# Loading q and k of the first batches by casting DMAs of GpSimd, with transposes by head and a new order up to block 2

## The chip, the core and the metric

The kernel runs on one core of a Trainium2 chip. The metric is device time in microseconds (us) of one launch. The engines are TensorE (PE in the profile; its weight loads are PEld), VectorE (DVE), ScalarE (ACT), GpSimd (POOL) and SyncE (SP, which only issues DMAs). A DMA can be issued from SP, ACT or POOL; only those issued from POOL are used here to change the type of the data on the way.

## The reference

q, k and v have the shape (8 batches, 8 heads, 576 positions, 64). Each head has two attentions, whose sum is the result; a two-layer network with an ELU follows on 4608 tokens of 512 values (512 to 2048 to 512).

```python
q_d = q.reshape(B, H, Sd, 4, D).mean(axis=3)      # k_d, v_d alike; Sd = 144
out_up = np.repeat(softmax_attention(q_d, k_d, v_d), 4, axis=2)
mask = np.abs(pos[:, None] - pos[None, :]) < 4
scores = np.where(mask, 0.125 * q @ k.T, -1e9)
out_local = softmax(scores) @ v
x = (out_up + out_local).transpose(0, 2, 1, 3).reshape(4608, 512)
h = x @ w_in
g = np.where(h > 0, h, np.exp(np.minimum(h, 0)) - 1)
out = g @ w_out
```

## The kernel before

Work on attention goes by batch b (8) and pair of heads j (4 pairs). For a pair, q and k are loaded as fp32 to 96 partitions by 2 heads by 6 runs by 64 (`load_qk`, lines 146 to 167), cast to fp16 with the two heads side by side (`cast_qk`), and transposed on PE in six chunks of 96 x 128, which puts one head on partitions 0 to 63 and the other on 64 to 127 of one PSUM tile (`transposes`, line 242). In batch 0 a further six matmuls with a constant matrix R (line 251) give the sums over four neighbours, that is the coarse q and k. PSUM goes to SBUF by `evict_q` (L264) and `evict_k` (L271) and, in batch 0, two small copies (L736, L737). From batch 3 on k is transposed by a DMA (`flip`) instead.

Then follow the scores (`masked_scores` in batch 0, which add a constant NEG on PE before ACT's exp at L338; `scores`, exp at L368 and a multiplication by MASK at L388 in later batches), the denominators (`den`, L403, L412, L444, L451), their spread over 128 partitions (`rb` in PSUM, L462 or L474, copied to `rcb`, L763 or L482), the sums of v (`vs`, L304), and the outputs (`lg`, L497 to L524), which DVE multiplies by the reciprocals (`ln`, L534 or L550). A last addition of the coarse to the fine part writes the token tile `xt` (L540 in batch 0, L570 later), on POOL or DVE by a list in the code.

The network goes over nine blocks of 512 tokens. MM1 of a block (`mm1`, L585 in block 0, L606 later) has sixteen steps: matmuls into `hp`, exp on ACT (`e`, L610), two instructions on DVE (L611, L612) that give `gt`. MM2 (`mm2`, L626) has sixteen steps too; its result leaves by ACT (L632) and SP.

The order of all of it is a list of events with due times written by hand: `at(time, fn, ...)` collects them, and a sort by time gives the program order, the same on every engine's queue. Only the order of the due times has a meaning. Batch 0 has its own table F (letters for T transposes, S and Z scores of the first and second half, D denominators, V sums of v, P spreads, O outputs, N normalising, H the part of MM1 that runs ahead, lv and lw the loads of v of batches 0 and 1, cv the casts of v, rp the loads of q and k of batch 1, wi the loads of w_in, k late constants) and FK, which counts filler matmuls on zeros (`keep`, L645, L648). Batches 1 to 3 have a table PLAN. MM1 and MM2 of blocks 0 to 3 have a start and a step each.

Events that share an engine wait for each other in that order: a DMA issue that waits for a free buffer holds up every later issue of its engine. `two` hands out PSUM slots of two banks in turn: three of them up to `close_front`, then two. In batch 0 `tq` and `tk` share the two slots of `misc`, so that the transposes of a pair wait until the pair before is evicted.

At the start (`first`, lines 650 to 664) SP issues q of pair 0 and q and k of pairs 1 and 2 of batch 0; ACT issues the identity ID, k of pair 0 and R; POOL issues NEG. q and k of pair 3 come later from SP. Pair 0 is cast in halves by ACT and DVE, and the six casts of pairs 1 to 3 are shared out by a list: q and k of pair 1 on ACT, q of 2 on POOL, k of 2 on DVE, q of 3 on POOL, k of 3 on ACT. In batch 1 all eight casts are on POOL, each with a small separating copy behind it (`apart`, L172).

Of the kernel before, what the change touches and what calls it, by code (L numbers as in the profile page):

```python
# [16 lines left out]
SD = S // 4  # L17
# [12 lines left out]
RUNS = 1  # L30
# [40 lines left out]
def kernel(  # L71
# [76 lines left out]
    def load_qk(b, j, held=False, queues=None):  # L148

        got = []  # L150
        for src, name in ((q, "q"), (k, "k")):
            a = src[b, 2 * j]
            t = sb.tile([QB, 2 * NB, D], FP32, tag=name + "32", bufs=3, name=name + "32")
            if held:
                nc.vector.memset(t[0:1, 0, 0:1], 0.0)
            runs_ = name == "q" or b < FLIP
            (nc.scalar if queues and name == "k" else nc.sync).dma_start(
                out=t[:].rearrange("p (e r) d -> p e (r d)", e=2) if runs_ else t[:],
                in_=bass.AP(
                    tensor=a.tensor, offset=a.offset,  # L160
                    ap=[[TPP * D, QB], [S * D, 2], [1, TPP * D]] if runs_
                    else [[D, QB], [QB * D, 2 * NB], [1, D]],
                ),
            )
            got.append(t)
        qk32[(b, j)] = got
# [7 lines left out]
    def cast_qk(b, j, half=False):  # L174

        got = []
        for t, name in list(zip(qk32.pop((b, j)), ("q16", "k16")))[:: 1 if b < FLIP else -1]:
            x = sb.tile([QB, NB, 2, D], FP16, tag=name, bufs=3, name=name)
# [4 lines left out]
            elif b == 0 and [2, 2, 0, 1, 0, 2][2 * j - 2 + (name == "k16")]:  # L183
                (act if [2, 2, 0, 1, 0, 2][2 * j - 2 + (name == "k16")] == 2 else dve)(out=x[:], in_=src)
            else:
                nc.gpsimd.tensor_copy(out=x[:], in_=src)  # L186
                apart(x[0:1, 0, 0, 0:1])
# [32 lines left out]
    def cast_v(b, j):  # L220
# [3 lines left out]
        if b >= RUNS:  # L224
            apart(v16[0:1, 0, 0, 0:1])
# [8 lines left out]
    def transposes(b, j, fill=(0, 0)):  # L234
# [3 lines left out]
        for x, t, name, n in zip(xs, tr_tiles(b), ("tq", "tk"), fill):  # L238
            s[name] = t
            keep(t, n)  # L240
            for c in range(NB):
                nc.tensor.transpose(  # L242
# [4 lines left out]
        if b == 0:  # L247
            for t in (s["tq"], s["tk"]):
                x = xs.pop(0)
                for c in range(TPP):  # L250
                    nc.tensor.matmul(
                        t[:, 736:1024].bitcast(FP32), x[:, c, :, :].rearrange("p e d -> p (e d)"),
                        C["R"][:, SD * (c // 2) : SD * (c // 2) + SD],
                        start=(c == 0), stop=(c == TPP - 1),
                    )
# [23 lines left out]
    def sums(b, j, x):  # L279
# [8 lines left out]
        if (b, j) == (1, 0) or (b >= RUNS and x == "k"):  # L288
# [241 lines left out]
    def normalise_half(js, g, lg):  # L530
# [7 lines left out]
        for t, a, b_, to in parts:  # L538
            eng = nc.vector if t == 0 and [0, 0, 0, 1, 0, 0, 0, 1][2 * g + js[0] // 2] else nc.gpsimd
# [6 lines left out]
    def normalise(b, j, lg):  # L546
# [14 lines left out]
        while t0 < S * (b + 1):  # L561
# [7 lines left out]
            eng = nc.vector if (b, t) == (1, 1) and [0, 0, 0, 1, 0, 0, 0, 1][4 + j] else nc.gpsimd  # L569
# [80 lines left out]
    def first():  # L650
# [116 lines left out]
    def first_v(j):  # L767
        v_first(0, j, dve if [0, 1, 0, 1][j] else act)
# [38 lines left out]
    F = dict(T=[-40.22, -40.16, -33.93, -33.13], S=[-38.63, -33.62, -33.34, -31.63], Z=[-32.71, -32.63, -32.4, -26.16], V=[-31.66, -30.84, -29.54, -26.17], P=[-29.55, -26.44, -25.1, -22.55], O=[-30.46, -25.6, -24.13, -20.55], N=[-25.77, -25.33, -22.75, -14.55], H=[-21.07, -20.28, -16.96, -14.76], lv=[-55.65, -54.27, -36.53, -31.7], cv=[-37.08, -33.24, -33.08, -27.13], lw=[-30.73, -29.44, -26.48, -13.01], rp=[-29.51, -28.21, -15.24, -13.2], D=[-32.62, -29.6, -25.74, -24.49], wi=[-33.23, -32.62, -30.61, -29.62], cf=[-27.76], k=[-54.63, -35.62, -30.55, -25.58], cq=[-54.5, -40.46, -33.4], l3=[-38.01])  # L807
    FK = dict(Tq=[1, 0, 0, 0], Tk=[0, 0, 0, 1], S=[0, 0, 3, 3], Z=[0, 0, 0, 0], P=[2, 2, 0, 3], O=[0, 0, 0, 0], D=[0, 1, 0, 0])
    for j in range(NPAIR):
# [12 lines left out]
        at(F["rp"][j], load_qk, 1, j, True)  # L822
        if j:
            at(F["cq"][j - 1], cast_qk, 0, j)
# [15 lines left out]
    MM1 = [[-14.36, 1.051, 0.555], [19.15, 0.992], [35.73, 1.022], [51.52, 1.02]]  # L840
    MM2 = [[14.98, 0.794], [34.5, 1.091], [51.68, 1.02]]
# [13 lines left out]
    def load(n):  # L855
# [14 lines left out]
    for b in range(1, B):  # L870
        p = PLAN[b]
        for j in range(NPAIR):
            n = NPAIR * (b - 2) + j
            at(p["cast"][j] - 0.1, cast_qk, b, j)
            at(p["cast"][j], cast_v, b, j)
            if b > 1:
                at(p["cast"][j] + 0.1, load, n + 3)
# [57 lines left out]
```

## Time and profile before

| | |
|---|---|
| time, median of 3 runs | 367.83 us (367.81 to 369.96) |
| profiled execution, its own time | 367.57 us |
| its span | 365.8 us |
| mean granted clock of PE | 0.967 |
| busy: PE, DVE, ACT, POOL | 343.8, 250.5, 201.2, 171.3 us |
| loads of q and k, median from issue to landing | 4.5 and 4.6 us |
| loads of w_in by GpSimd, the same | 8.2 us |

A row of the timeline or of a group names line, engine, operation and what it writes and reads (out<-in, partitions x elements). "Idle before, releaser" is the time that the engine stood still ahead of it and what ended that. The granted clock is a share of full speed. The DMA share can be over 1 for a stretch, since packets overlap.

### The profile page before, as it was taken

What the parts mean: (1) busy time and instruction counts of PE and PEld (TensorE: products, weight loads), DVE (VectorE), ACT (ScalarE), POOL (GpSimd) and SP (SyncE); (2) the same over time, 40 slices, a digit from 0 to 9 for tenths busy, and PEclk for the clock granted to TensorE, in tenths of its full rate; (3) what the DMA queues carried; (4) which work ended last, traced back from release to release, by engine and by line L of the source; (5) the groups of instructions that cost most, each with busy time, mean ns of one, the idle gap of its engine ahead of it and who ended that gap; (6) DMA issues with size and microseconds to landing.
All of it is one profiled execution on the core that took longest, in us unless ns stands there. A gap on an engine that the chain in (4) does not pass through costs nothing.

```text
span 365.8 us, 8655 instructions
## 1 busy us (share of the span) xinstructions
PE 343.8 (94%) x3394; PEld 196.0 (54%) x3394; DVE 250.5 (68%) x461; ACT 201.2 (55%) x369; POOL 171.3 (47%) x314
## 2 busy tenths in 40 slices
PE   6999788699978999999999999999999999999995
PEld 2766675465545555555555555555545544444443
DVE  1216799657787877987898789879865955555510
ACT  3474489417866576477547754764654343443421
POOL 0374788469593954792497449863410500000000
PEclk9579999969998999999999999999999999999999
DMA  8999999998798197688878797825004011001012
GB/s 205 201 173 221 221 207 219 218 197 219 164 205 183 35 239 158 146 187 187 174 165 187 162 204 164 193 68 110 30 30 116 30 46 40 30 37 49 30 59 85
DMA packets 100242, 51.17 MB, mean 140 GB/s; under 512 B 81770, under 2 KB 95178, under 8 KB 100202
## 3 DMA queue, kind: packets, MB, share of 16 engines
q1 hardware_dynamic: 97018, 45.90, 57.6%
q0 software_dynamic: 2736, 4.32, 6.8%
q8 instruction: 26, 0.43, 0.5%
q10 hardware_dynamic: 448, 0.40, 0.4%
q14 instruction: 14, 0.11, 0.1%
HBM read 42.24 MB, written 9.62 MB: 142 GB/s over the span
## 4 chain that ended last, share of the span: by engine, by line
PE 82%; DVE 9%; ACT 3%; DMA 2%; issue 2%; POOL 1%; SPq 0%; DVEq 0%; ACTq 0%
PE op L626 33%; PE hp L606 29%; PE sc L348 3%; PE hp L585 2%; PE lg L497 2%; DMA k<-in_k_dram 2%; PE tqk L242 2%; DVE gt L612 2%; DVE e L611 2%; POOL xt L570 1%; DVE pex L388 1%; ACT pex L368 1%; PE den L403 1%; DVE ln L550 1%; PE vs L304 1%
## 5 line engine op out<-in xcount | busy, mean ns | idle before, releaser
L626 PE MATMUL op<-WO,gt 128*128 128x512 f16 (+2 forms) x592 | 145.8, 375 | 0.0
L610 ACT ACTIVATE e<-hp 128x512 f16<-128x512 f32 x144 | 86.4, 602 | 101.2 <-PE hp L606 87.7
L606 PE MATMUL hp<-xt,WI 128*128 128x512 f16 x512 | 133.5, 383 | 0.6 <-POOL xt L570 0.3
L612 DVE SCALAR_TENSOR_TENSOR gt<-hp,e 128x512 f16<-128x512 f32 x144 | 99.6, 692 | 6.5
L611 DVE TENSOR_SCALAR e<-e 128x512 f16<-128x512 f16 x144 | 62.4, 433 | 44.5 <-ACT e L610 43.9
L626 PEld LDWEIGHTS <-gt 128*128 128x128 f16 x592 | 55.3, 98 | 60.9 <-issue 0.6
L606 PEld LDWEIGHTS <-WI 128*128 128x128 f16 x512 | 55.4, 115 | 49.6 <-issue 1.8
L570 POOL TENSOR_TENSOR xt<-ln 128x128 f16<-128x128 f16 (+10 forms) x62 | 37.1, 629 | 52.8 <-DVE ln L557 41.2
L368 ACT ACTIVATE pex<-sc 112x576 f16<-112x576 f32 x112 | 50.0, 530 | 13.7 <-PE sc L358 13.6
L388 DVE TENSOR_TENSOR pex<-pex,MASK 112x1152 f16<-112x1152 f16 x28 | 23.8, 849 | 15.7 <-ACT pex L368 15.7
L295 POOL TENSOR_TENSOR t<-qt 128x288 f32<-128x288 f16 x27 | 18.0, 666 | 33.7 <-ACT qt L264 33.7
L186 POOL CAST q<-q 96x768 f16<-96x768 f32 x30 | 24.7, 824 | 14.7 <-DMA q<-in_q_dram 10.5
L632 ACT COPY os<-op 128x512 f32<-128x512 f32 (+2 forms) x37 | 21.4, 579 | 18.0 <-PE op L626 17.9
L223 POOL CAST v<-v 112x768 f16<-112x768 f32 x32 | 27.1, 846 | 4.1 <-DMA v<-in_v_dram 4.1
L186 POOL CAST k<-k 96x768 f16<-96x768 f32 x28 | 23.5, 839 | 0.3
L289 DVE TENSOR_REDUCE kd<-kt 128x144 f16<-128x576 f16 x28 | 20.8, 744 | 0.7 <-ACT kt L271 0.7
L264 ACT COPY qt<-tqk 128x576 f16<-128x576 f16 x28 | 18.1, 646 | 4.5 <-PE tqk L242 4.0
L585 PE MATMUL hp<-xt,WI 128*128 128x256 f16 x128 | 15.9, 273 | 2.7 <-DVE gt L612 1.8
L348 PEld LDWEIGHTS <-kt 64*112 64x112 f16 x336 | 11.0, 128 | 12.7 <-issue 11.1
L242 PEld LDWEIGHTS <-q 96*128 96x128 f16 x192 | 12.1, 102 | 8.9 <-issue 3.9
L348 PE MATMUL sc<-qt,kt 64*112 64x96 f16 x336 | 14.8, 219 | 1.3 <-ACT kt L271 1.3
L585 PEld LDWEIGHTS <-WI 128*128 128x128 f16 x128 | 13.5, 114 | 3.3 <-issue 2.9
(104 smaller groups left out, 302.3 us busy)
## 6 DMA issues: line engine op xcount, KB each, us to landing
v<-in_v_dram SPq DMA_DIRECT2D x30, 336.0 KB, 6.3
q<-in_q_dram SPq DMA_DIRECT2D x32, 288.0 KB, 4.5
out_dram<-os SPq DMA_DIRECT2D x35, 256.0 KB, 2.1
k<-in_k_dram SPq DMA_DIRECT2D x31, 288.0 KB, 4.6
rcb<-rd SPq DMA_DIRECT2D x10, 360.0 KB, 5.4
WI<-in_moe_w_in_dram POOLq DMA_DIRECT2D x4, 512.0 KB, 8.2
WO<-in_moe_w_out_dram POOLq DMA_DIRECT2D x4, 512.0 KB, 8.1
v<-in_v_dram SPq DMA_DIRECT2D x2, 308.0 KB, 6.1
```

The lines of the kernel that those rows point to most:

```text
L186: nc.gpsimd.tensor_copy(out=x[:], in_=src)
L223: nc.gpsimd.tensor_copy(out=v16[:], in_=v32[:].rearrange("p (e c) d -> p c e d", e=2))
L348: nc.tensor.matmul(sc[e][0:KW, a : a + QB], s["kt"][r, KO - PAD + QB * c :][:, 0:KW], s["qt"][c][r], start=True, stop=True,)
L368: nc.scalar.activation(out=s["p"][0:rows, e, :, a : a + n], in_=g2(sc[0:rows], a, n), func=AF.Exp, scale=SCALE / 16 if b and a == HB else ...
L388: nc.vector.tensor_tensor(out=to, in0=to, in1=mk2, op=AB.mult)
L570: eng.tensor_tensor(out=xt(t)[:, j, t0 - TBLK * t : t1 - TBLK * t], in0=ln[:, la : la + z - a], in1=_rep4(ln[:, ga : ga + (z - a) // 4]), ...
L585: nc.tensor.matmul(FS[i][:, 256 * f : 256 * f + 256], w_in(dc, 2 * n + f), xts[0][:, dc, 256 * h : 256 * h + 256], start=(f == dc == 0), s ...
L606: nc.tensor.matmul(hp, w_in(dc, fc), xts[t][:, dc, :], start=(dc == 0), stop=(dc == DMC - 1),)
L610: nc.scalar.activation(out=e, in_=hp, func=AF.Exp)
L611: nc.vector.tensor_scalar(out=e, in0=e, scalar1=1.0, scalar2=-1.0, op0=AB.min, op1=AB.add)
L612: nc.vector.scalar_tensor_tensor(out=to, in0=hp, scalar=0.0, op0=AB.max, in1=e, op1=AB.add)
L626: nc.tensor.matmul(op_[:, a:z], gts[t][:, fc, 128 * tt : 128 * tt + 128], WO[:, fc, a:z], start=(fc == 0), stop=(fc == FCN - 1),)
```

## The change

The six tensors q and k of pairs 1 to 3 of batch 0, and all eight of batch 1, are loaded by DMAs that POOL issues and that write fp16. Such a DMA keeps the two heads one behind the other in a partition, so the pair is transposed head by head: 12 transposes of 96 x 64 into one half of the partitions each in place of 6 of 96 x 128, and in batch 0 the same for the sums by R. The casts of these tensors go. Pair 0 of batch 0 is handled as before, but k is issued from SP, and NEG is loaded by SP rather than POOL. The fp16 tiles have four buffers instead of three. Three of four xt additions of block 0's first parts are on DVE in place of one, all four copies of vd on ACT in place of two, and there are 13 fillers at the start for 12. The due times of batches 0 to 3 are new.

```diff
+    def runs_of(src, b, j):
+        a = src[b, 2 * j]
+        return bass.AP(
+            tensor=a.tensor, offset=a.offset, ap=[[TPP * D, QB], [S * D, 2], [1, TPP * D]]
+        )
+    def by_head(x):
+        return x[:].rearrange("p c e d -> p (c e d)").rearrange("p (e n) -> p e n", e=2)
+    def is_cast(b, j):
+        return b < 2 and (b, j) != (0, 0)
+    def load_cast(b, j):
+        qk16[(b, j)] = []
+        for src, name in ((q, "q16"), (k, "k16")):
+            x = sb.tile([QB, NB, 2, D], FP16, tag=name, bufs=4, name=name)
+            nc.gpsimd.dma_start(out=by_head(x), in_=runs_of(src, b, j))
+            qk16[(b, j)].append(x)
...
+                if is_cast(b, j):
+                    for e in range(2):
+                        nc.tensor.transpose(
+                            t[64 * e : 64 * e + 64, 128 * c : 128 * c + QB],
+                            by_head(x)[:, e, D * c : D * c + D], C["ID"][0:QB, 0:QB],
+                        )
+                    continue
...
+                    for e in range(2):
+                        nc.tensor.matmul(
+                            t[64 * e : 64 * e + 64, 736:1024].bitcast(FP32),
+                            by_head(x)[:, e, D * c : D * c + D], sums_of_4,
+                            start=(c == 0), stop=(c == TPP - 1),
+                        )
...
-            eng = nc.vector if t == 0 and [0, 0, 0, 1, 0, 0, 0, 1][2 * g + js[0] // 2] else nc.gpsimd
+            eng = nc.vector if t == 0 and [1, 1, 1, 0, 0, 0, 0, 1][2 * g + js[0] // 2] else nc.gpsimd
...
-        keep(t, 12)
+        keep(t, 13)
         const(id_np, "ID", nc.scalar)
-        for j in range(NPAIR - 1):
-            load_qk(0, j, queues=(j == 0))
+        load_qk(0, 0)
+        for j in range(1, NPAIR):
+            load_cast(0, j)
         const(sums_np, "R", nc.scalar)
-        const(neg_np, "NEG", nc.gpsimd)
+        const(neg_np, "NEG", nc.sync)
...
-        v_first(0, j, dve if [0, 1, 0, 1][j] else act)
+        v_first(0, j, dve if [0, 0, 0, 0][j] else act)
...
-    F = dict(T=[-40.22, -40.16, -33.93, -33.13], S=[-38.63, -33.62, -33.34, -31.63], Z=[-32.71, -32.63, -32.4, -26.16], V=[-31.66, -30.84, -29.54, -26.17], P=[-29.55, -26.44, -25.1, -22.55], O=[-30.46, -25.6, -24.13, -20.55], N=[-25.77, -25.33, -22.75, -14.55], H=[-21.07, -20.28, -16.96, -14.76], lv=[-55.65, -54.27, -36.53, -31.7], ...)
+    F = dict(T=[-41.13, -39.95, -36.66, -32.16], S=[-39.2, -35.63, -33.39, -30.84], Z=[-32.52, -32.14, -32.14, -28.4], V=[-33.32, -30.92, -30.71, -27.94], P=[-29.75, -28.02, -20.88, -18.53], O=[-30, -26.95, -20.73, -13.92], N=[-28.12, -24.72, -19.09, -13.8], H=[-24.18, -20.45, -18.09, -17.91], lv=[-52.45, -36.44, -34.49, -32.17], ...)
-    FK = dict(Tq=[1, 0, 0, 0], Tk=[0, 0, 0, 1], S=[0, 0, 3, 3], Z=[0, 0, 0, 0], P=[2, 2, 0, 3], O=[0, 0, 0, 0], D=[0, 1, 0, 0])
+    FK = dict(Tq=[1, 0, 0, 0], Tk=[0, 0, 2, 0], S=[1, 0, 2, 1], Z=[1, 0, 2, 0], P=[0, 1, 0, 0], O=[1, 4, 0, 2], D=[0, 0, 0, 0])
...
-        at(F["rp"][j], load_qk, 1, j, True)
-        if j:
-            at(F["cq"][j - 1], cast_qk, 0, j)
+        at(F["rp"][j], load_cast, 1, j)
...
-    MM1 = [[-14.36, 1.051, 0.555], [19.15, 0.992], [35.73, 1.022], [51.52, 1.02]]
+    MM1 = [[-14.19, 1.09, 0.706], [19.14, 0.992], [35.73, 1.018], [51.52, 1.02]]
...
-        1: dict(tr=[-8.501, -7.483, -3.079, -0.967], sc=[-4.069, -1.465, 0.547, 3.047], cast=[-21.27, -19.9, -10.3, -4.149], dn=[16.3], vs=[18.33], sp=[18.62, 18.82, 18.27, 18.69], out=[18.9, 18.88, 18.82, 18.95], ...),
+        1: dict(tr=[-12.21, -5.594, -1.76, -1.482], sc=[-7.07, 0.103, 0.888, 2.276], cast=[-23.96, -13.31, -12.32, 1.701], dn=[16.38], vs=[15.62], sp=[18.61, 18.14, 18.46, 18.98], out=[18.98, 18.52, 18.54, 18.99], ...),
...
-    at(F["l3"][0], load_qk, 0, 3)
-    for n, x in enumerate([-7.269, -2.453, 5.077]):
+    for n, x in enumerate([-8.454, -6.202, 3.581]):
         at(x, load, n)
```

MM2 of block 0 has the due times 14.98 + 0.794 i before and after; the due times of batches 2 and 3, of w_in and of w_out move by less.

More of the change, by code (lines that the diff above doesn't have):

```diff
@@ L29 @@
 KG, CG = 96, 24
-RUNS = 1
 KO = 16
@@ L156, in load_qk @@
             runs_ = name == "q" or b < FLIP
-            (nc.scalar if queues and name == "k" else nc.sync).dma_start(
+            nc.sync.dma_start(
                 out=t[:].rearrange("p (e r) d -> p e (r d)", e=2) if runs_ else t[:],
@@ L177, in cast_qk @@
         for t, name in list(zip(qk32.pop((b, j)), ("q16", "k16")))[:: 1 if b < FLIP else -1]:
-            x = sb.tile([QB, NB, 2, D], FP16, tag=name, bufs=3, name=name)
+            x = sb.tile([QB, NB, 2, D], FP16, tag=name, bufs=4, name=name)
             src = t[:].rearrange("p (e c) d -> p c e d", e=2)
@@ L182, in cast_qk @@
                 dve(out=x[:, :, 1, :], in_=src[:, :, 1, :])
-            elif b == 0 and [2, 2, 0, 1, 0, 2][2 * j - 2 + (name == "k16")]:
-                (act if [2, 2, 0, 1, 0, 2][2 * j - 2 + (name == "k16")] == 2 else dve)(out=x[:], in_=src)
             else:
@@ L287, in sums @@
         src = s["q"][:, 0:S] if x == "q" else s["kt"][:, KO : KO + S]
-        if (b, j) == (1, 0) or (b >= RUNS and x == "k"):
+        if (b, j) == (1, 0) or x == "k":
             nc.vector.tensor_reduce(
@@ L568, in normalise @@
             la, ga = (a + SH * h, HB + HB * h + a // 4) if by_pe(b) else (a, S + a // 4)
-            eng = nc.vector if (b, t) == (1, 1) and [0, 0, 0, 1, 0, 0, 0, 1][4 + j] else nc.gpsimd
+            eng = nc.vector if (b, t) == (1, 1) and [1, 1, 1, 0, 0, 0, 0, 1][4 + j] else nc.gpsimd
             eng.tensor_tensor(
@@ L838, in spread @@
         spread_copy(b, j, rb, copy)
-    MM1 = [[-14.36, 1.051, 0.555], [19.15, 0.992], [35.73, 1.022], [51.52, 1.02]]
-    MM2 = [[14.98, 0.794], [34.5, 1.091], [51.68, 1.02]]
+    MM1 = [[-14.19, 1.09, 0.706], [19.14, 0.992], [35.73, 1.018], [51.52, 1.02]]
+    MM2 = [[14.98, 0.794], [34.5, 1.095], [51.68, 1.02]]
     def mm1_at(t, i):
@@ L873 @@
             n = NPAIR * (b - 2) + j
-            at(p["cast"][j] - 0.1, cast_qk, b, j)
             at(p["cast"][j], cast_v, b, j)
             if b > 1:
+                at(p["cast"][j] - 0.1, cast_qk, b, j)
                 at(p["cast"][j] + 0.1, load, n + 3)
@@ L892 @@
                 at(p["out"][js[0]], pair_outputs, b, js)
-    at(F["l3"][0], load_qk, 0, 3)
-    for n, x in enumerate([-7.269, -2.453, 5.077]):
+    for n, x in enumerate([-8.454, -6.202, 3.581]):
         at(x, load, n)
-    for n, x in enumerate([-16.78, -5.044, -1.229, -0.973]):
+    for n, x in enumerate([-21.48, -3.996, 1.576, 2.844]):
         at(x, load_wo, n)
```

24 lines of the change are left out of this document (13 added, 11 removed).

## The prediction

> **What bounds the kernel now.** I read the busy times by stage first, to see where TensorE is not the limit. The columns are the stretch, its length, busy time (and instructions) of PE, PEld, DVE, ACT and POOL, the granted clock, the DMA share and GB/s.
>
> ```profile
> 50.00:60.00 10.00, 8.14 (x106) 6.79 (x103) 9.37 (x21) 9.64 (x22) 9.49 (x17) 1.00 0.98 201
> 60.00:80.00 20.00, 15.44 (x245) 9.91 (x246) 13.89 (x21) 8.49 (x16) 11.22 (x22) 0.83 1.16 218
> 80.00:100.00 20.00, 19.79 (x164) 10.53 (x164) 15.02 (x24) 14.10 (x28) 15.43 (x31) 1.00 0.85 194
> 100.00:366.00 266.00, 258.02 (x2298) 136.27 (x2296) 189.54 (x332) 142.91 (x263) 110.23 (x203) 0.99 0.50 115
> ...
> 8.00:9.00 1.00, 0.24 (x6) 0.13 (x4) 0.23 (x2) 0.49 (x1) 0.00 (x0) 0.74 1.10 270
> 22.00:23.00 1.00, 1.00 (x21) 1.00 (x20) 0.00 (x0) 0.31 (x2) 1.00 (x2) 0.94 1.26 210
> 74.00:76.00 2.00, 1.91 (x45) 1.69 (x46) 1.00 (x2) 0.76 (x1) 0.09 (x1) 0.50 1.34 190
> ```
>
> From 80 us on PE works nearly without a gap (19.79 of 20, then 258.02 of 266): what comes after 80 us is a fixed length, and the end moves only as far as its start moves. The edits lie before that. There, at 50 to 60 us, DVE (9.37), ACT (9.64) and POOL (9.49) are all full and PE is not; at 60 to 80 us PE loses 4.56 us and part of its clock. At the very start the clock falls within 8 to 9 us and is back only within 22 to 23 us.
>
> Then the chain that ended last, in order of time (start, length, what), for what sets the start:
>
> ```profile
> 1.69 7.60 DMA k<-in_k_dram
> 9.31 0.83 ACT k L184
> 10.14 0.53 ACT qt L264
> 11.56 0.64 PE tq L242 x6
> ```
>
> The load of k of pair 1 lands at 9.29. ACT casts it, and the eviction of pair 0 (L264 to L737) stands behind that cast in ACT's order and takes to 11.56, some 1.4 us. PE can start pair 1 only then, when pair 0's two PSUM tiles are free. From there PE has work without a break (1.00 of 1.00 still in the row at 22 us), so a time won at 11.56 is passed on.
>
> **The change, part by part.** *The start.* Rows of the timeline (start, length, engine, line; what ended the idle time), the bytes of 2 to 5 us, and one load on GpSimd's queue with its time to landing:
>
> ```profile
> 1.20 4.65 PE L645 MATMUL sc<-Z 128*128 128x512 f16 x12 [1.20 <-DVE v L652]
> 7.25 0.51 ACT L181 CAST k<-k 96x384 f16<-96x384 f32 x1 [1.75 <-DMA k<-in_k_dram]
> 9.06 0.88 PE L251 MATMUL tq<-R,q 96*128 96x144 f16 x6 [0.82 <-DMA R<-Rc]
> 1.23 0.70 POOL L89 DMA_DIRECT2D NEG<-NEGc  x1 [0.78 <-POOLq L919]
> ...
> DMA packets 671, 0.82 MB, mean 273 GB/s; under 512 B 158, under 2 KB 669, under 8 KB 671
> ...
> NEG<-NEGc POOLq DMA_DIRECT2D x1, 126.0 KB, 6.6
> ```
>
> Before, k of pair 0 shares the engines with q and k of pairs 1 and 2 on SP and lands at 7.2; R is queued behind it on ACT and lands at 9.06. Afterwards only q and k of pair 0 (by their shapes 288 KB each), ID (24.5) and R (81) are ahead, some 680 KB, and 820 KB had moved by 5 us here: I take k and R at about 5.3. The casting loads come later on their own: NEG, issued at 1.23, landed 6.6 us on, at 7.8. So PE ends its 12 fillers at 5.85 as before and the 13th at about 6.1, transposes q and k by 6.8 and has summed q by R at 7.4 (by the starts shown in the next fence); ACT then takes its 1.4 us with no cast ahead and frees the tiles at 8.9. q and k of pair 1 are issued at 1.2 and 1.9; with NEG's 6.6 us they land at 7.8 and 8.5, a little more with v beside them: 9.3. **PE starts pair 1 at 9.3 instead of 11.56, 2.2 us earlier.** Bounds: if R and k land as before, eviction starts at 9.8 rather than 10.05 (0.3 us); if the loads are no limit, 2.7.
>
> The casts of pairs 1 to 3 of batch 0 go (three on ACT at 0.83, one on DVE, two on POOL). SP no longer waits for a free fp32 buffer before the last q and k, so v comes earlier, and with it the loads of WI that stand behind the casts of v in POOL's order. The six issues of about 0.7 us lie on a POOL that does nothing yet (0.00 in the row at 8 us). NEG moves to SP and delays v by its 126 KB, half a microsecond at 273 GB/s, which SP's missing wait gives back.
>
> *Transposes and sums by head.* Pairs 1 to 3 of batch 0 and all of batch 1 issue twice the instructions, each for 64 output partitions. Whether two run side by side is seen in the output matmuls, which write halves too:
>
> ```profile
> 27.49 0.32 PE L517 MATMUL lg<-pex,v 112*64 112x96 f16 x6
> 27.64 0.23 PE L524 MATMUL lg<-pex,vd 96*64 96x72 f16 x4
> 44.11 0.42 PE L242 MATMUL tqk<-ID,q 96*128 96x96 f16 x6
> 44.37 0.42 PE L242 MATMUL tqk<-ID,k 96*128 96x96 f16 x6
> 12.20 0.48 PE tk L242 x6
> 12.68 0.72 PE tq L251 x6
> ...
> L517 PEld LDWEIGHTS <-v x48: 106/108/111, 27.5 to 36.2; 112*64 112x64 f16 x48
> L242 PEld LDWEIGHTS <-q 96*128 96x128 f16 x192 | 12.1, 102 | 8.9 <-issue 3.9
> ```
>
> Six halves of 96 columns take 0.15 us from start to next start (27.49 to 27.64), 25 ns each; six full ones 0.26 (44.11 to 44.37), 43 ns each. A pair of halves, 50 ns, so costs 7 more than one full: 12 halves 0.30 for 0.26. Fourteen tiles of transposes and six of sums at 0.04 are 0.8 us; batch 1's eight lie in a stretch where PE isn't the limit. I take **+0.5 us**. Low end 0. High end, one after another: at the low clock 0.48 a tile of transposes and 0.72 a tile of sums (12.20 and 12.68), 2.4 a pair, 7.2 for three pairs. [...]
>
> *DVE in the front.* Three of the four xt adds go to DVE instead of one; two copies of vd (0.42 each) go to ACT.
>
> ```profile
> L540 DVE TENSOR_TENSOR xt<-ln 128x448 f16<-128x448 f16 x1 | 1.2, 1194 | 0.0
> L570 DVE TENSOR_TENSOR xt<-ln 128x288 f16<-128x288 f16 x1 | 0.8, 755 | 0.0
> L680 DVE CAST vd<-vs 96x256 f16<-96x256 f32 x2 | 0.8, 420 | 3.4 <-PE vs L304 3.4
> L611 DVE TENSOR_SCALAR e<-e 128x512 f16<-128x512 f16 x16 | 7.4, 463 | 1.4 <-ACT e L610 1.4
> L186 POOL CAST q<-q 96x768 f16<-96x768 f32 x30 | 24.7, 824 | 14.7 <-DMA q<-in_q_dram 10.5
> ...
> 34.32 2.56 POOL L540 TENSOR_TENSOR xt<-ln 128x576 f16<-128x576 f16 x3
> 31.53 0.89 DVE L534 TENSOR_TENSOR ln<-lg,rcb 128x720 f16<-128x720 f32 x1
> 39.47 0.29 DVE L611 TENSOR_SCALAR e<-e 128x512 f16<-128x512 f16 x1 [0.74 <-ACT e L610]
> ```
>
> By the line through 288 (0.755) and 448 (1.194) elements one of 576 is 1.55: 2 x 1.55 + 1.19 - 1.19 - 0.84 = +2.3 us of DVE. Between the first ln at 31.53 and the first e at 39.47 DVE is nearly full. But the second add no longer waits for POOL (34.32, nearly 2 us after its ln), and the last ln and add now stand behind the first block of MM1 in the order, so they no longer precede e. I take **+0.7 us**, bounds -1 and +2.3.
>
> *The middle, 40 to 66 us.* POOL loses eight casts of 0.82 us (the row of L186) with their separators, over 6.6 us, and gets eight issues earlier, beside its waits for ln. The e of DVE takes 463 ns on the mean but 0.28 to 0.29 when undisturbed (39.47): 16 times the difference is 2.8 us of a full DVE, in the stretch where POOL casts nearly all the time. With two of three casts of batch 1 gone I take **-1.0 us**; bounds 0 and -2.8. What is late next there is DVE's own work, which stays.
>
> *The tail of batch 1.* These rows show the passage from MM2 of block 0 to MM1 of block 1:
>
> ```profile
> 65.58 0.66 PE L403 MATMUL den<-pex,IND 112*32 112x144 f16 x29 [1.24 <-DVE k L155]
> 68.06 1.78 ACT L368 ACTIVATE pex<-sc 112x576 f16<-112x576 f32 x4 [4.35 <-PE sc L358]
> 70.21 0.63 PE L304 MATMUL vs<-v,VR 112*32 112x128 f16 x24
> 71.81 0.62 PE L474 MATMUL rb<-rc,FOUR 16*128 16x144 f16 x12 [0.97 <-DVE rcb L482]
> 70.86 0.90 DVE L482 CAST rcb<-rb 128x720 f16<-128x720 f32 x1
> 74.93 1.89 DVE L550 TENSOR_TENSOR ln<-lg,rcb 128x720 f16<-128x720 f32 x2 [1.70 <-PE lg L505]
> 79.90 0.92 PE L606 MATMUL hp<-xt,WI 128*128 128x512 f16 x3 [0.28 <-POOL xt L570]
> ```
>
> Now all four spreads (rb) and the sums of v (vs) turn in two PSUM slots before the first outputs; the first ln is at 74.93, and the xt adds crowd behind it up to 79.90. The new due times put vs ahead of the denominators and order spread 1, 2, outputs 1, 2, spread 0, outputs 0, spread 3, outputs 3. With the first spread near 70, the copies of pairs 1 (ACT) and 2 (DVE) end by 71.8, and the first ln starts there, 3 us earlier; the other two pairs follow at a copy and an ln of 0.9 each, so the last ln ends near 77, and MM1 of block 1, at 79.90 today, can follow its xt adds some 2 us earlier. The last scores of batch 1 are also put ahead of the last MM1 block, which takes some of the 1.24 us before den. Against it: MM2 of the stretch is moved, not removed. I take **-2.2 us**; bounds -3.5 and +0.5. This holds only if ACT is free for pair 1's copy; today its exps end at 69.84 (68.06 + 1.78).
>
> Sum: -2.2 + 0.5 + 0.7 - 1.0 - 2.2 = -4.2 on the profiled execution, 367.57 us (span 365.8 and 1.77 around it): 363.4. The median of the runs shown is 367.83, 0.26 above it: **363.6**.
>
> **Rivals.** *The clock (faster).* It fell in the 8-to-9 row after PE had been idle most of 6 to 9 us, and came back at 22, although PE was full from 12 on. If PE is busy to 7.6 and again from 9.3, it may stay up or return one step sooner; the time at half clock, 8.5 to 22.1 by the shares in those two rows, is four steps of 3.4 us, if there are steps, and at half clock a step costs 1.7 us. Two steps: 363.6 - 3.4 = 360.2. One later: 365.3. [...] Against the gain: what PE does there, full for ten microseconds, did not bring the clock back. Chance 0.1.
>
> *Swallowed by DVE and ACT (no change).* If the adds cost 2.3 and DVE, full from 40 to 66 us, keeps its pace, only part of the start arrives: -2.2 + 0.5 + 2.3 - 1.0 on the front and -0.5 at the tail, 366.9. For it speaks 9.37 of 10 in 50 to 60 us. Chance 0.22.
>
> *GpSimd's queue late (no change).* If six loads on one queue queue up behind each other and v's many small packets, pair 1 starts at 12 to 13 instead of 9.3: 366.3 to 367.3. It decides when k of pair 1 lands after 11.5. Chance 0.1.
>
> *Halves one after another (slower).* 7.2 us instead of 0.5 on PE's unbroken stretch from 9.3: 370.3, and with batch 1's eight tiles at 0.26 uncovered, 372.4. It decides if a tile of 12 halves takes over 0.5 us at full clock. Against it stands 27.49 to 27.64; but that row has no transposes. Chance 0.1.
>
> **How the numbers follow.** Forecast (361.4 to 365.8) 0.48, and the rivals 0.1, 0.22, 0.1, 0.1. One per cent of 367.83 is 3.7 us, about what a measurement of this kernel can tell from no change; so faster lies below 364.15. Of the forecast 0.36 lies there, with the clock 0.46; the halves give 0.06 above 371.5 and a tail turned wrong together with late loads 0.08; the rest, 0.40, is within. The range is 360.0 to 369.0: it leaves out the serial halves and half of the clock's case.
>
> **What would show it.** The first per-head transposes near 9.3 us and no cast on ACT but pair 0's; 12 halves in 0.3 us at full clock; first e of MM1 near 37; e nearer to 0.3 us at 40 to 55; first ln of batch 1 within 7 us of its denominators and fewer half-clock slices near 75. I am wrong if pair 1 waits for a load on GpSimd's queue, if the xt adds on DVE delay e, or if the stretch from the denominators to MM1 of block 1 stays at 14 us.

## The result and the profile after

The changed kernel took 357.80 us (median of four runs, 356.68 to 358.49) against 368.89 for the kernel before beside it: ratio 0.9695, 95% interval 0.9646 to 0.9744. In three later series it gave 0.9779 (0.9740 to 0.9818), 0.9767 (0.9704 to 0.9829) and 0.9772 (0.9712 to 0.9833); that is 8.1 to 8.6 us below the kernel before by the ratio, and 8.1 to 10.3 us between the medians. All times and ratios below are of fast runs; one run of e3 (365.85 us) and one of the kernel before in the last series (572.52 us) were slow and are left out. The forecast was 363.6 with a range of 360.0 to 369.0: right in sign, with 4.2 us of gain where 8 to 11 were measured, and the range ended above the measured time.

The profiled execution took 356.68 us (span 354.8). Starts in the two profiles, in us:

| | before | after | won so far |
|---|---|---|---|
| first transposes of pair 1 | 11.56 | 9.66 | 1.9 |
| first ln of batch 0 | 31.53 | 26.56 | 5.0 |
| first e of MM1 | 38.84 | 35.75 | 3.1 |
| denominators of batch 1, first whole tile | 64.09 | 60.73 | 3.4 |
| first ln of batch 1 | 74.93 | 66.95 | 8.0 |
| MM1 of block 1 | 79.90 | 72.09 | 7.8 |
| denominators of batch 2 | 103.0 | 95.0 | 8.0 |
| end of the span | 365.8 | 354.8 | 11.0 |

Single executions differ: in three further profiles of the changed kernel (e5, e12 and e16 below) pair 1 starts at 8.8 to 9.5, the first ln comes at 24.2 to 24.8, the first e at 33.4 to 37.1, and MM1 of block 1 starts at 70.4 to 73.6.

Rows of the changed kernel's timeline for most of the right-hand starts:

```profile
8.25 0.64 ACT L298 COPY qt<-tq 128x576 f16<-128x576 f16 x1 [2.13 <-PE tq L279]
9.66 0.45 PE L263 MATMUL tq<-ID,q 96*64 96x96 f16 x12 [1.07 <-ACT qd L771]
9.91 0.45 PE L263 MATMUL tk<-ID,k 96*64 96x96 f16 x12
...
35.75 1.08 ACT L644 ACTIVATE e<-hp 128x512 f16<-128x512 f32 x2 [1.99 <-PE hp L619]
60.73 0.68 PE L437 MATMUL den<-pex,IND 112*32 112x144 f16 x32
66.95 1.72 DVE L584 TENSOR_TENSOR ln<-lg,rcb 128x720 f16<-128x720 f32 x2
72.09 0.81 PE L640 MATMUL hp<-xt,WI 128*128 128x512 f16 x3
```

The start came near its forecast (9.66 for 9.3), and twelve halves take 0.25 us (9.66 to 9.91). The place of the third gain, from 60.73 to 66.95, was forecast too. Not forecast were the front's 5 us at ln, 2 of which are gone again at the first e, and the last 3 us, which appear only after 95 us.

By stage, the kernel before first, then the changed one (columns as in the first fence of the prediction):

```profile
40.00:66.00 26.00, 21.01 (x275) 17.99 (x278) 23.75 (x50) 19.80 (x40) 20.99 (x39) 1.00 1.09 220
66.00:82.00 16.00, 13.55 (x210) 8.61 (x199) 9.18 (x11) 5.35 (x9) 9.43 (x19) 0.79 1.16 202
100.00:130.00 30.00, 26.00 (x326) 15.07 (x325) 23.43 (x36) 19.00 (x37) 22.27 (x43) 0.94 0.71 147
```

```profile
40.00:66.00 26.00, 24.07 (x360) 17.96 (x357) 21.08 (x46) 21.62 (x44) 15.83 (x29) 1.00 1.03 210
66.00:82.00 16.00, 14.07 (x176) 8.53 (x174) 12.74 (x18) 7.81 (x15) 13.19 (x26) 1.00 1.05 217
100.00:130.00 30.00, 28.42 (x345) 16.18 (x343) 24.58 (x42) 20.23 (x38) 19.45 (x37) 1.00 0.79 164
```

POOL falls from 20.99 to 15.83 us at 40 to 66, and PE rises by 3. At 100 to 130 us PE stood still for 4.0 us before and for 1.6 after: a stage that the prediction had taken for full.

The granted clock over the 40 slices of the page, before and after:

```profile
PEclk9579999969998999999999999999999999999999
```

```profile
PEclk9998999999999999999999999999999999999999
```

Counted by microsecond, the half clock took 11.94 us of TensorE's time before (8.5 to 22, 73 to 80, 110.6 to 114) and 1.71 after (31.4 to 34.6).

### The profile page after: what moved, and what is told of

It reads as the page before. It is cut to its first block, busy times and chain, and to the rows that moved or that the text cites. A ratio compares the mean times of both kernels' runs of the same rounds, so it can differ in the third digit from the quotient of the medians.

```text
span 354.8 us, 8863 instructions
## 1 busy us (share of the span) xinstructions
PE 338.6 (95%) x3520; PEld 191.6 (54%) x3520; DVE 247.1 (70%) x452; ACT 200.0 (56%) x368; POOL 167.6 (47%) x305
## 3 DMA queue, kind: packets, MB, share of 16 engines
q0 software_dynamic: 5600, 6.26, 10.6%
## 4 chain that ended last, share of the span: by engine, by line
PE 88%; DVE 5%; ACT 4%; issue 2%; DVEq 0%; ACTq 0%
PE op L660 35%; PE hp L640 31%; PE sc L382 3%; PE lg L531 2%; PE hp L619 2%; PE sc L679 2%; PE tqk L268 2%; ACT pex L402 1%; PE sc L392 1%; PE vs L338 1%; DVE ln L584 1%; DVE gt L646 1%; PE lg L539 1%; PE den L437 1%; ACT e L644 1%
## 5 line engine op out<-in xcount | busy, mean ns | idle before, releaser
L640 PE MATMUL hp<-xt,WI 128*128 128x512 f16 x512 | 132.0, 380 | 0.7 <-DVE xt L604 0.6
L645 DVE TENSOR_SCALAR e<-e 128x512 f16<-128x512 f16 x144 | 60.1, 417 | 40.2 <-ACT e L644 39.5
L640 PEld LDWEIGHTS <-WI 128*128 128x128 f16 x512 | 55.0, 114 | 48.2
L402 ACT ACTIVATE pex<-sc 112x576 f16<-112x576 f32 x112 | 50.0, 528 | 10.6 <-PE sc L392 10.5
L323 DVE TENSOR_REDUCE kd<-kt 128x144 f16<-128x576 f16 x28 | 20.8, 744 | 1.1 <-ACT kt L305 1.1
L205 POOL CAST k<-k 96x768 f16<-96x768 f32 x24 | 20.4, 848 | 0.1
L205 POOL CAST q<-q 96x768 f16<-96x768 f32 x24 | 19.7, 821 | 0.2 <-issue 0.2
L619 PE MATMUL hp<-xt,WI 128*128 128x256 f16 x128 | 17.0, 283 | 0.5 <-DVE v L217 0.4
L331 POOL TENSOR_TENSOR qd<-t 128x144 f16<-128x144 f32 x27 | 14.0, 519 | 2.1
L591 DVE TENSOR_TENSOR ln<-lg,rcb 128x576 f16<-128x576 f32 x20 | 15.0, 748 | 0.0
```

The lines of the kernel that those rows point to most:

```text
L402: nc.scalar.activation(out=s["p"][0:rows, e, :, a : a + n], in_=g2(sc[0:rows], a, n), func=AF.Exp, scale=SCALE / 16 if b and a == HB else ...
L619: nc.tensor.matmul(FS[i][:, 256 * f : 256 * f + 256], w_in(dc, 2 * n + f), xts[0][:, dc, 256 * h : 256 * h + 256], start=(f == dc == 0), s ...
L640: nc.tensor.matmul(hp, w_in(dc, fc), xts[t][:, dc, :], start=(dc == 0), stop=(dc == DMC - 1),)
L645: nc.vector.tensor_scalar(out=e, in0=e, scalar1=1.0, scalar2=-1.0, op0=AB.min, op1=AB.add)
```

## The experiments

Ratios are to the kernel before, with their 95% interval; kernels measured in one series on one chip share the runs of it (e1 to e4, e5 to e8, e9 to e12, e13 to e16, e17 and e18). "Changed" is the changed kernel; its three later ratios are those above, 0.977 on the mean. A difference to the kernel before is worked out from the ratio, one between two edited kernels from their medians. Each quoted text below is what was expected before the run.

### The loads against the order

*New loads, old order* (e3: the old F, FK, PLAN, MM1, MM2, engine lists and 12 fillers in the changed kernel) and *old loads, new order* (e4: `is_cast` False everywhere, fp32 loads and casts as before).

> Casting loads and work by head as in the changed kernel, but the due times, the fillers, and the lists of engines of the kernel before. Theory CLOCK: pair 1 starts near 9.7 us and the front gains what the clock allows, 361 to 365; a drop of the clock near 74 stays, as its order is the old one. Theory ORDER: the loads alone are worth 2 us at most, 366 to 368.

> The due times, fillers and lists of engines of the changed kernel, but all loads of q and k, their casts and the transposes of both heads at once as in the kernel before (casts of batch 1 at their old due times). Theory CLOCK: the clock falls in the front as before and stays up in the tail of batch 1; 362 to 366. Theory ORDER: the order keeps most of its gain, 358.5 to 361.5.

e3: 361.17 us (three runs, 359.35 to 362.99), 0.9870 (0.9809 to 0.9930). e4: 362.70, 0.9892 (0.9853 to 0.9930). Either alone gives about half, 4.8 and 4.0 us of 366.23; the sum, 8.8, is the whole, within the intervals. Both times lie in the range of theory CLOCK and not in that of ORDER, but the clock did not do what CLOCK says: in e4, with the old loads, it stayed up to 33 us and fell near 74. The prediction had 2.7 for the loads (-2.2 + 0.5 - 1.0) and 1.5 for the order (+0.7 - 2.2): both came out smaller than these; for the loads the interval (2.6 to 7.0) just reaches 2.7. In e4 TensorE also waited, in the middle of the front:

```profile
28.27 0.63 PE L621 MATMUL hp<-xt,WI 128*128 128x256 f16 x4
33.64 1.02 PE L621 MATMUL hp<-xt,WI 128*128 128x256 f16 x4 [3.90 <-DMA WI<-in_moe_w_in_dram]
```

### Which loads

*Batch 1's loads old* (e9) and *batch 0's loads old* (e10) in the changed kernel, and *batch 1's loads new in the kernel before* (e17). The core of the edits:

```diff
-        return b < 2 and (b, j) != (0, 0)
+        return b == 0 and j > 0          # e9: batch 1 by load_qk and cast_qk
+        return b == 1                    # e10 and e17: batch 0 as before
```

> The changed kernel with q and k of batch 1 loaded in fp32 by SP and cast by GpSimd (its transposes one whole matrix each again); batch 0 and the order stay changed. The loads alone had brought some 4.8 us. Theory A (GpSimd's eight casts in the middle are what the loads save: they stand ahead of its xt adds and of the transposes of batch 1): 2 to 3 us above the changed kernel of the same call, the middle from the first e to the denominators of batch 1 at 26 to 28 us instead of 25. Theory B (all the gain of the loads is in the start of batch 0): within 1 us of the changed kernel.

> The changed kernel with q and k of pairs 1 to 3 of batch 0 loaded in fp32 by SP and the ACT queue, cast by ACT, DVE and GpSimd as before; batch 1 and the order stay changed. Theory A (the start is worth what the prediction said, 2.2 us, and it is passed on): pair 1's transposes at 11 to 12 us and 2 to 3 us above the changed kernel of the same call. Theory B (a start that comes sooner is met by the loads of w_in or by another wait before the first block): pair 1 at 11 to 12 us, but the first e not more than 1 us later and the time within 1 us.

> The kernel before with q and k of batch 1 alone by casting DMAs of GpSimd (issued where their loads were issued, halves transposed by themselves); batch 0 and the whole order stay as before. Both new loads in the old order had given 4.1 us, and in the new order leaving out batch 1's cost 3.8 and batch 0's 2.6. Theory A (batch 1's casts on GpSimd are the larger part in any order): 2 to 4 us less than before. Theory B (in the old order those casts lie in cover, and the loads gain by batch 0 alone): within 1 us of before.

e9: 360.93, 0.9859 (0.9804 to 0.9914), 3.8 us above the changed kernel of its series (e12: 357.09, 0.9704 to 0.9829); by the ratios it is 3.4, some 3 either way. e10: 359.71, 0.9809 (0.9758 to 0.9861), 2.6 above, or 1.5 by the ratios, which is not told apart from zero. e17: 364.41, 0.9941 (0.9898 to 0.9985), 2.2 us (0.6 to 3.7) below the kernel before. So the estimates for batch 1's casts are 2 to 4 us in either order, where the prediction took 1.0; neither interval by itself leaves 1.0 out. The waits of TensorE between 36 and 67 us (engine and line; releaser: us, times, longest), first in e9, then in the kernel before:

```profile
PE sc L382 <- ACT pex L402: 1.3, 2, 0.6
PE tqk L268 <- POOL q L205: 1.1, 1, 1.1
PE tqk L268 <- POOL k L205: 0.9, 2, 0.6
```

```profile
PE hp L585 <- DVE gt L612: 1.8, 2, 1.6
PE tqk L242 <- ACT pex L368: 1.6, 2, 1.1
PE sc L348 <- ACT kt L271: 1.3, 2, 0.7
PE den L403 <- DVE k L155: 1.2, 1, 1.2
PE hp L585 <- issue: 1.0, 1, 1.0
```

In e9 the transposes of batch 1 wait 2.0 us for POOL's casts, and the stretch from the first e to the denominators of batch 1 takes 28.8 us, in which one piece of half clock (40 to 44 us, 1.7 us of loss) falls as well; in the four profiles of the changed kernel it takes 25.0 to 25.6 and has no such wait. That is how the casts cost time in the new order. In the kernel before no wait for POOL stands among these rows, and the stretch takes 25.3 us (38.84 to 64.09), in e17 26.5. How the casts cost time in the old order is open. In e10 pair 1 begins at 10.58 instead of 8.8 to 9.7, and TensorE then waits 2.3 us for w_in.

### The order, piece by piece

The *changed kernel again* (e5), with the *old order of batch 1's tail* (e6), with the *old PLAN of batches 2 and 3* (e7), and with the *old order, fillers and engine lists of batch 0* (e8).

```diff
-        1: dict(... dn=[16.38], vs=[15.62], sp=[18.61, 18.14, 18.46, 18.98], out=[18.98, 18.52, 18.54, 18.99], ...)
+        1: dict(... dn=[16.3], vs=[18.33], sp=[18.62, 18.82, 18.27, 18.69], out=[18.9, 18.88, 18.82, 18.95], ...)   # e6
```

> The changed kernel again, on the same chip as the three that follow, so that they have their comparison. Both theories: 0.9695 of before as measured, 355 to 358.5.

> The changed kernel with the old due times of denominators, sums of v, spreads and outputs of batch 1 alone. Theory TAIL (the new order of this tail keeps PE busy enough that the clock does not fall near 74, and is worth over 3 us with the clock): from den to the first MM1 of block 1 it takes 13 to 15 us instead of 11.4, the clock falls there, time 3 to 4 us above the changed kernel. Theory FRONT (the tail was slow because what came before it was late; the order by itself is worth what the prediction gave it): 1 to 2.2 us above.

> The changed kernel with the old due times of batches 2 and 3 alone. From the first MM1 of block 1 to the end the time was 285.9 us before and 282.7 after. If the new order of batch 2's spreads and outputs is the cause: 2 to 3 us above the changed kernel, with a fall of the clock near 104. If the cause is the clock's windows or loads: within 1 us of it.

> Casting loads and the new due times from batch 1 on, but the old due times and fillers of batch 0 and the old lists of engines (xt adds, vd copies). With all due times old the first e of MM1 came at 33.6 us in one execution, against 35.8 in the changed kernel. Theory FRONT: the new order of batch 0 is part of the gain, 2 us or more above the changed kernel. Rival: the front's gain is the loads' alone, 1 us below to 1 us above it.

e5: 358.83, 0.9779, less of a gain than the 0.9695 expected. e6: 360.62, 0.9819 (0.9781 to 0.9858). e7: 360.60, 0.9825 (0.9771 to 0.9880). e8: 357.96, 0.9755 (0.9705 to 0.9804). The old tail costs 1.8 us, the old plan of batches 2 and 3 costs 1.8 too, and the old order of batch 0 nothing. Each difference is known to some 2 us only, so neither 1.8 is clear of zero by its time; the profiles support the first two. From the denominators of batch 1 to MM1 of block 1, e6 takes 15.4 us and e5 11.4 (before 15.8, after 11.4). Over all twenty profiles this stretch takes 11.4 to 12.8 us in the thirteen with the new order of the tail and 13.3 to 15.8 in the seven with the old one. From there to the end of the span it takes 282.7 to 284.9 us in the thirteen with the new plan of batches 2 and 3 and 285.5 to 287.3 in the seven with the old one. At 100 to 130 us, e7 and then e5:

```profile
100.00:130.00 30.00, 27.37 (x319) 15.39 (x318) 23.44 (x38) 18.48 (x35) 20.24 (x39) 0.89 0.75 163
```

```profile
100.00:130.00 30.00, 29.07 (x336) 16.37 (x336) 23.34 (x38) 18.43 (x35) 18.95 (x37) 0.89 0.82 163
```

At the same clock, the old plan leaves TensorE idle for 2.6 us there and the new one for 0.9. The fall of the clock near 104 that was expected of e7 came in e5 too (102 to 110 us), so it does not tell the two apart.

### The clock in the front

*Three fillers for 13* in the changed kernel (e1) and *24 for 12* in the kernel before (e2): `keep(t, 3)` and `keep(t, 24)`.

> The changed kernel with 3 fillers at the start instead of 13, nothing else. Theory CLOCK (most of the gain is TensorE's granted clock: 24 us at half clock before, 3 us after): PE is cold at 8 us, the front runs at half clock to about 20 us, first e of MM1 3 us or more after 35.75, time 360 to 364. Theory ORDER (the gain comes from the order, the loads and the freed engines, and the clock costs little because PE waits for others there anyway): within 1 us of 357.8.

> The kernel before with 24 fillers at the start instead of 12, so that PE is busy to about 8.4 us while q, k and R are still on their way. Theory CLOCK: the clock does not fall at 8.5 us or falls for a shorter time, the front is 2 to 4 us shorter, time 364 to 366.5. Theory ORDER: 367.5 to 369.5, since fillers change no order and no load.

e2: 365.65, 0.9997 (0.9968 to 1.0025). The page of e2:

```profile
PEclk9999699989998999999999999999999999999999
```

The clock stays up to 36 us, the first ln of batch 0 comes at 26.85 instead of 31.53, and nothing is won: TensorE then stands still for 3.06 us at 31.8 with no releaser shown, and the half clock comes at 36 to 43 instead. The time lies in the range of theory CLOCK only because the kernel before beside it took 366.23; the ratio is what ORDER says. One profile proves little here: e14 below, which has 12 fillers, kept the clock up to 28 us as well. But the ten runs of e2 have a mean granted clock of 0.980 against 0.968 in the fifteen of the kernel before beside them, at the same time.

e1: 359.96, 0.9838 (0.9803 to 0.9873), some 2.4 us worse than the changed kernel's 0.977, which lies outside this interval (the intervals of that kernel's later series reach into it). The time is at the lower end of theory CLOCK, but the first e came at 36.02, not 3 us late. Two windows of PE alone (the granted clock stands behind PE's busy time) and four rows of the timeline of e1 hold a surprise:

```profile
8.00:12.00 4.00, 3.00 (x49) 1.00 1.30 197
12.00:16.00 4.00, 4.00 (x55) 1.00 1.08 178
```

```profile
10.18 0.92 PE L285 MATMUL tq<-R,q 96*64 96x144 f16 x12
10.89 0.93 PE L285 MATMUL tk<-R,k 96*64 96x144 f16 x12
...
22.38 0.54 PE L285 MATMUL tq<-R,q 96*64 96x144 f16 x12
22.75 0.54 PE L285 MATMUL tk<-R,k 96*64 96x144 f16 x12
```

The granted clock is 1.00. Yet twelve sums take 0.71 us (10.18 to 10.89) where they take 0.37 twelve microseconds later. TensorE runs at about half speed until 20.8 us and no column of the clock tells it; only the distance of equal groups does. The first ln is 5.2 us later than in a control (29.36 against 24.18 in e12), and about half of that reaches the end.

### Where the sooner front goes: the last quarter of w_in

In ten profiles with the new order of the front or the new loads, the second group of MM1's first block waited, for 0.4 to 5.8 us. In e4 and e10 the profile names w_in, in the others nothing. The rows of e16, a third control: the last quarter's issue, the first two groups, and, from the view of that issue, its time to landing.

```profile
20.87 0.75 POOL L137 DMA_DIRECT2D WI<-in_moe_w_in_dram  x1
...
28.02 0.63 PE L619 MATMUL hp<-xt,WI 128*128 128x256 f16 x4
33.59 1.02 PE L619 MATMUL hp<-xt,WI 128*128 128x256 f16 x4 [4.09 <-issue]
```

```profile
DMA to landing us min/median/max: 12.6/12.6/12.6
```

20.87 + 12.6 is 33.47, and the group starts at 33.59. In all ten it starts 0.05 to 0.13 us after the last quarter has landed, although by the code it reads the first quarter alone: steps 0 and 1 take columns 0 to 511 of WI, first for K chunk 0, then for chunk 1. Chunk 1's part of these columns lies in the tile behind chunk 0's part of all the other quarters. Two edits test it, one that delays the last two quarters (e11), one that cuts the four loads by K chunk (e13, and e14 in the kernel before):

```diff
-    F = dict(... wi=[-33.19, -32.56, -30.01, -29.05], ...)
+    F = dict(... wi=[-33.19, -32.56, -27.0, -25.0], ...)                                     # e11
-        nc.gpsimd.dma_start(out=WI[:, :, a:z], in_=src)
+        c = a // 512
+        nc.gpsimd.dma_start(out=WI[:, c, :], in_=moe_w_in[128 * c : 128 * c + 128, :])       # e13, e14
```

> The changed kernel with the last two quarters of w_in issued some 3 and 4 us later in the order, so that the first two have the DMA engines to themselves. Theory A (the first block of MM1 waits for w_in, and TensorE's unexplained stalls of 1 to 4 us at 23 to 34 us come of the same full DMA engines): first two quarters land 2 to 4 us earlier, stalls before the first e below 0.5 us, first e at 33 to 34 us, 1 to 2.5 us less than the changed kernel of the same call. Theory B (the stalls are not set by w_in): the stalls stay, first e at 35 to 37 us, time within 1 us, or slower by up to 3 if the last quarters now come late.

> The changed kernel itself, for the differences of this call: a ratio of 0.970 to 0.980 to the kernel before by every theory, with a first e between 35 and 37.5 us by the length of TensorE's stalls at 23 to 34 us.

> The changed kernel with the four loads of w_in cut by rows (one K chunk of WI each, contiguous in the tile) instead of by columns; same bytes, same places in the order. In seven runs the second group of the first MM1 block (K chunk 1) began 0.05 to 0.13 us after the LAST quarter had landed. Theory A (the group waits for quarters it doesn't read, because its columns lie inside the span of every later quarter in the tile): with rows it needs the second load alone; no stall over 0.5 us before it, first e at 32 to 34.5 us and spread less from run to run, 1 to 3 us less than the changed kernel. Theory B (the stall is instructions that come late, and the match is chance): a stall of 1 to 5 us before the second group as before, time within 1 us of the changed kernel.

> The kernel before with the same cut of w_in by rows. There the last quarter landed at 34.6 us and the first group of MM1 began at 35.4, with nothing waiting for it. Theory A (it is the sooner front of the changed kernel that runs into w_in): no change, within 1 us of before. Theory B (w_in by rows is faster whoever uses it, by its long runs): 1 us or more less than before, and the last load lands in clearly less than 10.9 us.

e11: 362.31, 0.9890 (0.9837 to 0.9942), 5.2 us above its control e12 (357.09): the expectation that the first quarters matter was wrong, the stall grew to 5.82 us. (In e12 the first e came at 33.44, sooner than the 35 to 37.5 expected.) The same rows of e11, the landing being that of the two late issues:

```profile
25.34 1.51 POOL L137 DMA_DIRECT2D WI<-in_moe_w_in_dram  x2
...
35.44 1.02 PE L619 MATMUL hp<-xt,WI 128*128 128x256 f16 x4 [5.82 <-issue]
```

```profile
DMA to landing us min/median/max: 6.9/8.1/9.3
```

The second of the two issues, at some 26.1, lands 9.3 us later, at 35.4. e13 takes the wait away:

```profile
28.13 0.62 PE L619 MATMUL hp<-xt,WI 128*128 128x256 f16 x4
29.52 0.63 PE L619 MATMUL hp<-xt,WI 128*128 128x256 f16 x4
30.31 0.60 PE L619 MATMUL hp<-xt,WI 128*128 128x256 f16 x4
31.12 0.63 PE L619 MATMUL hp<-xt,WI 128*128 128x256 f16 x4 [0.20 <-DMA WI<-in_moe_w_in_dram]
...
34.39 0.45 PE L263 MATMUL tqk<-ID,k 96*64 96x96 f16 x12 [1.45 <-DMA k<-in_k_dram]
```

The groups follow each other and the first e comes at 31.56 (33.4 to 37.1 in the four profiles of the changed kernel). That the group waited for a quarter it doesn't read is shown; that the program's waits go by the span of a load in the tile is my reading of why. But e13's time is 357.10, 0.9769 (0.9716 to 0.9822), the same as its control e16 (358.08, 0.9772): transposes of batch 1 now wait 2.1 us for k, scores 1.3 us for POOL, and the denominators come at 58.3 against 59.0 in the best control. e14: 366.27, 0.9961 (0.9926 to 0.9996): in the kernel before, where the last quarter landed at 34.6 and the first group began at 35.35, the cut is worth 1.4 us (0.1 to 2.7). That is what theory B gave it, but the last load took 11.0 us, no less than the 10.9 of before, so why it helps there is open.

Two last kernels ask whether more is to be had. *Old front order, rows, and the first q and k of batch 1 two places earlier* (e15), and *24 fillers and rows in the kernel before* (e18).

> New loads, the new order from batch 1 on, but the old order and engines of batch 0; w_in by rows; and the first q and k of batch 1 issued two places earlier, since with the old order the transposes of batch 1 waited 3.0 us for that k. Theory A (the front is held by these two transfers alone): both waits gone, first e at 31 to 32.5 us, 2 to 5 us less than the changed kernel. Theory B (the DMA engines are full until 40 us, so a transfer put first makes another late): a wait of 1 to 3 us for w_in or for another load turns up in its place and the time is within 1 us of the changed kernel.

> The changed kernel itself, for the differences of this call: 0.970 to 0.980 of before. If the second group of the first MM1 block waits, it begins within 0.15 us of the landing of the last quarter of w_in (theory A of the run with w_in by rows); if it waits and begins at another time, theory B.

> The kernel before with 24 filler matmuls instead of 12, so that the clock stays up in the first 22 us, and with w_in cut by rows, so that no group waits for a quarter it doesn't read. The fillers alone changed nothing (ratio 0.9997), the rows alone 0.9961. Theory A (the clock in the front is worth some 3 us, and w_in's last quarter had swallowed it): 2 to 5 us less than before. Theory B (the front is set by the data and by the other engines, whatever the clock): within 1.5 us of before.

e15: 357.57, 0.9769 (0.9729 to 0.9809): no wait for w_in or k is left, a first e at 33.56, and the time of the changed kernel. e18: 364.23, 0.9934 (0.9893 to 0.9976), by the ratio 2.4 us below before (0.9 to 3.9), which reaches into both theories: with w_in out of the way the clock in the front is worth perhaps 1 us over the rows alone, which the intervals don't part. No kernel here beat the changed one by more than the measurement tells.

## Why the prediction was wrong, point by point

The step that failed most plainly is the one that took what comes after 80 us as a fixed length, a term of nothing where 1.8 us were won. Next to it the middle was sized at -1.0 where the estimates are -2 to -4, and two costs (+0.5 and +0.7) did not show.

**The start, -2.2: right in place, about half of it the loads' own.** Pair 1 began at 9.66, 1.9 us earlier, with ACT's copies at 8.25 and no cast ahead of them; it waited for these copies, where the prediction had it wait for its own load. In four other profiles with the old loads of batch 0 (e4, e10, e14, e17), in which the clock was still up at 9 us, pair 1 began at 10.3 to 10.6, and in the four of the changed kernel at 8.8 to 9.7: 1.2 us on the mean. The rest goes with the half clock that the profile of before has from 8.5 us on. The step "a time won at 11.56 is passed on" did not hold in full: it holds as far as the first MM1 groups, where the last quarter of w_in ends the wait (2.1 to 4.4 us in three of four profiles of the changed kernel). What batch 0's loads are worth in the end, 1.5 to 2.6 us in e10, is not told apart from zero.

**Halves, +0.5: its low end, nothing.** Twelve halves take 0.25 us at full clock (9.66 to 9.91) where six whole transposes took 0.26. The price of 25 ns for a half, read from another kind of matmul, was some 4 ns too high; the rival of serial halves is out.

**DVE in the front, +0.7: mis-sized, and of no weight.** Three rows of the changed kernel's groups on DVE up to 67 us, by form:

```profile
L645 DVE TENSOR_SCALAR e<-e 128x512 f16<-128x512 f16 x16 | 4.8, 303 | 0.1
...
L574 DVE TENSOR_TENSOR xt<-ln 128x576 f16<-128x576 f16 x2 | 1.5, 757 | 0.1
...
L574 DVE TENSOR_TENSOR xt<-ln 128x448 f16<-128x448 f16 x1 | 0.6, 627 | 0.0
```

The adds take 0.757 and 0.627 us, not 1.55 and 1.19: the row of before that priced them (37.54 to 38.73) ran beside a cast on POOL (37.43 to 38.25). In e8 the old lists and order of the front cost nothing, 0.9 us less than its control.

**The middle, -1.0: the term that was mis-sized among the loads.** e did fall from 463 to 303 ns (first row above; 297 to 393 in the four profiles), as the step said. But leaving the casts in cost 3.8 us (e9), with e at 533 ns and 2.0 us in which transposes wait for POOL's casts, which the step put aside; taking them out alone gave 2.2 (e17), with e at 406 ns. In e9 TensorE waits for POOL and hardly for DVE, in the kernel before for DVE's gt (1.8 us) and not for POOL, so which of the two carries the gain is shown for the new order alone. POOL at 9.49 of 10 in the stage's own row should have been priced as a possible wait: of the 6.6 us of eight casts a third (e17) to somewhat over a half (e9) arrived.

**The tail, -2.2: right in place and size.** The first ln of batch 1 came 6.2 us after its denominators, and undoing the order cost 1.8 us (e6). The profile shows twice that, 4.4 us; two windows of half clock fell into this stretch before and none after, which may be the rest.

**"What comes after 80 us is a fixed length": wrong, a miss of 1.8 us.** From MM1 of block 1 to the end 285.9 us became 282.7, and undoing the plan of batches 2 and 3 alone cost 1.8 us (e7). Over all profiles the new plan takes 1.9 us less there on the mean (284.2 and 286.1), and no profile of the one lies among those of the other. The row that carried the claim averaged over 266 us; drawn by 30 us, it has 26.00 busy of 30 at 100 to 130, the very stage that the edits of batch 2 reach.

Together, the pieces undone one by one: loads 4.8, tail 1.8, batches 2 and 3 1.8, front order 0, that is 8.4, against 8.1 to 8.6 by the ratio in the three series that held both kernels. Each piece has some 2 us either way, so the agreement is partly luck. The 11.1 of the first comparison has a kernel before that was 1.4 to 2.7 us slower than in the later series; why is open.

**The clock rival (0.1): half right.** The half clock did go from the front, and from other places, seven windows to one. The rival's step is in the profile of before: the loss of 6.82 us between 8.5 and 22 us is four pieces of 3.41 us at half clock, 1.71 us of loss each. But in the kernel before a clock held up changed nothing (e2), so by itself it does not make the gain. It is not without weight either: with TensorE at half speed up to 20.8 us the changed kernel was some 2.4 us slower (e1). How much of the gain hangs on the clock is open. Among the 16 runs of the changed kernel, worked out from their mean clock, those with one window average 355.99 us and those with four 359.25, about 1.1 us a window; since the profiles with the longest stalls for w_in have more windows too (4.1 and 4.4 us with three and four, in e16 and e5; 0 and 2.1 us with one, in after and e12), this is a relation and not a price.

## What to carry to other kernels

Before a stage is called full, cut its row to the length that the edit reaches: 258 of 266 hid 4 us in 30. A helper engine that is full in a stage and feeds the others can be a bound of that stage: the work taken from it is to be priced as a wait, and not only by what it does to its neighbours. A stall for which the profile names no releaser is to be held against the landing times of all transfers; here it was a load that the waiting matmul doesn't read, and cutting the loads the way the reader walks the tile took it away, though other waits filled its place and the time stayed (357.10 and 358.08 us).

## What the hardware showed

- *The half clock comes in equal pieces.* In all twenty profiles, up to 350 us, the loss is a multiple of 1.71 us, that is of 3.41 us at half clock (0.50 in the rows of single microseconds): one piece (after, e12, e13) to seven (before, e17). Steady work alone did not bring the speed back in e1: TensorE was full from 10 us on, with transposes and small sums, and kept half speed until 20.8 us (twelve sums in 0.71 us at 10.18 and at 15.42, in 0.37 at 22.38), with 1.00 in the column of the granted clock.
- *Landing times swing.* The last quarter of w_in took 9.3 us (e11) to 13.9 us (e5) from issue to landing, with a DMA share above 1 (1.24 at 23 to 40 us in e12). Of the four profiles of the changed kernel, the two in which the second group waited little (0 and 2.1 us) took 356.68 and 354.98 us, the two in which it waited 4.1 and 4.4 took 359.56 and 360.04.
- *A stop inside a group is open.* In nine profiles of kernels with the changed order, the changed kernel's four among them, TensorE stops for 0.6 to 2.0 us after two of eight equal sums (L485, "issue"), always at the same instruction (e1, e4 and e10, which have that order too, don't stop there):

```profile
28.92 0.21 PE L485 MATMUL den<-pex,IND 96*32 96x72 f16 x2
31.09 0.30 PE L485 MATMUL den<-pex,IND 96*32 96x72 f16 x6 [1.96 <-issue]
```

In the changed kernel one packet of instructions (0.02 MB) moved between 28 and 29 us, just ahead of the stop in these rows, but in the kernel before one moved in the same microsecond without a stop; that the stop is a wait for instructions is a guess that no run here tested.
